# Queries and keys of batches 2 to 7: transposed by DMA instead of TensorE, with the bias columns appended to their token rows

## The chip, the cores and the metric

One core of one Trainium2 chip. The metric is the device time of one execution in microseconds (us). Every ratio below is the mean time of one kernel's fast runs over the mean of the other's fast runs of the same rounds, so it is not quite the ratio of the medians that are quoted beside it. "Fast" excludes executions in the chip's slower state. The "granted clock" is the share of TensorE's full clock that the profile shows as granted.

## The reference, cut to what matters

```python
# q, k, v: (8 batches, 8 heads, 576 tokens, 64);  s: (8, 8, 576)
scores = q @ k.T / 8
cum    = cumsum(max(s, 0))                       # per head, over tokens
bias   = min(-(cum[i] - cum[j]), 0)              # query i, key j
attn   = softmax(where(j > i, -1e9, scores + bias))
x      = concat_heads(attn @ v)                  # (8, 576, 512)
out    = x + relu(layernorm(x) * g @ w1) @ w2    # 512 -> 2048 -> 512
```

The bias is a difference of two vectors, so it can be carried by the score product itself: keys get the columns (c_hi, c_mid, c_lo, 1) and queries (1, 1, 1, -c), and the contraction grows from 64 to 68.

## The kernel before: the parts concerned

Everything runs as one software pipeline over n = 0 to 63, one step per head (n = 8 x batch + head). In each step TensorE (PE in the profile) does the scores of head n, the product with v of head n-1, and four "units" of the feed-forward network of the previous batch. Scores need q and k with the head dimension on the partitions; both arrive with tokens there, so they are transposed. In the kernel before TensorE does it, two heads at a time, and VectorE (DVE) copies the result from PSUM:

```python
def qk_pair(b, j):
    for kind, dst in (("k", kT), ("q", qT)):
        src = ready.pop((kind, b, j))                          # 96 x (6 x 2 x 64), bf16
        tr = ps_t.tile([P, S], BF16, name="trqk", tag="tr")    # ps_t: 2 buffers, tag "tr"
        for t in range(QT):                                    # 6 transposes
            nc.tensor.transpose(tr[:, t*QP:(t+1)*QP], src[0:QP, t], ident[0:QP, 0:QP])
        for u in range(2):                                     # 2 copies of 64 x 576
            copy_on("dve", dst[i][0:D, hh+u, 0:S]..., tr[u*D:(u+1)*D, :]...)

def aug(b, g, eng):            # the bias rows: four small DMAs per group of four heads
    for j, src in enumerate((c_hi, c_mid, c_lo)):
        eng.dma_start(out=kT[i][D+j:D+j+1, :, 0:S], in_=src[r0:r0+G, :])
    eng.dma_start(out=qT[i][D+3:D+4, :, 0:S], in_=c_neg[r0:r0+G, :])
# ... cut ...
def ln_tr(b, t):               # LayerNorm's own transposes use the same two PSUM buffers
    tr = ps_t.tile([P, KD, P], BF16, name="trx", tag="tr")
    ...
```

At the start of a batch, in the step of head 1, LayerNorm of the batch before stands on VectorE: statistics, reciprocal root (on GpSimd, POOL in the profile), five tiles xn, and then trx on TensorE. The output rows go out by

```python
def put(yo):
    nc.sync.dma_start(out=out[b, t*P:(t+1)*P, :], in_=yo)      # on SyncE's queue, at once
```

SyncE (SP, its queue SPq) issues all loads and stores, in program order (in the timeline of the changed kernel below, a store whose data is not there holds what stands behind it for 3.5 us).

The softmax here doesn't subtract the row's maximum and nothing guards it: scores larger than these inputs give would overflow.

## Time and profile before

| | before |
|---|---|
| time, median of the first three runs | 445.18 us (444.15 to 446.87) |
| span of the profiled run, mean granted TensorE clock | 445.4 us, 0.971 |
| TensorE / VectorE / ScalarE / GpSimd busy | 85 / 63 / 39 / 38% |
| DMA queue of SyncE, share of the 16 engines | 37.0% |
| a batch, first head to first head (batches 3 to 7) | 46.3 us |

A busy share is an average over the span; what sets the pace is read from how far apart the same instruction of successive heads lies, and from the waits of the engine that is full. Those views stand in the prediction.

### The profile page before, as it was taken

The page shows a single profiled execution, that of the slowest core. Times are in us where ns is not written, and L with a number is a line of the kernel's source. Part 1 is how long each engine was busy: PE and PEld are TensorE (multiplying, and loading weights), DVE is VectorE, ACT ScalarE, POOL GpSimd, SP SyncE. Part 2 cuts the span into 40 slices and gives each one's busy share as a digit, 9 for nine tenths or more (in the row PEclk, how much of TensorE's full clock was granted, in tenths as well). Part 3 has the DMA queues.
Part 4 walks back from the last instruction along what each step waited for, and adds up shares of the span by engine and source line. Part 5 has one row for each costly group of instructions (what it writes and reads, how often), then busy time and mean ns, then how long its engine had stood idle before and what let it go on. Part 6 is the DMA issues. An engine that isn't in the chain of part 4 may idle for free.

```text
span 445.4 us, 8185 instructions
## 1 busy us (share of the span) xinstructions
PE 377.6 (85%) x2973; PEld 208.6 (47%) x3024; DVE 280.8 (63%) x615; ACT 174.1 (39%) x339; POOL 171.4 (38%) x415
## 2 busy tenths in 40 slices
PE   1396459995999799969998899889997999999995
PEld 0174335553555455535554455445554554444442
DVE  8668787597656865775576767766668676411211
ACT  4164216631275136612762265215642560140420
POOL 4166514865445444442555255524444222000000
PEclk9999999997999899988999999969999999999999
DMA  7887075964531354134511551154221000101013
GB/s 198 214 231 199 10 243 174 271 197 119 143 107 55 101 149 115 29 96 129 142 56 52 162 152 54 53 149 125 71 76 47 26 1 24 72 0 72 24 26 71
DMA packets 61593, 47.13 MB, mean 106 GB/s; under 512 B 40232, under 2 KB 52784, under 8 KB 61552
## 3 DMA queue, kind: packets, MB, share of 16 engines
q1 hardware_dynamic: 61472, 46.56, 37.0%
q8 instruction: 24, 0.39, 0.4%
q14 instruction: 17, 0.14, 0.1%
q10 hardware_dynamic: 80, 0.05, 0.0%
HBM read 36.85 MB, written 9.44 MB: 104 GB/s over the span
## 4 chain that ended last, share of the span: by engine, by line
PE 65%; DVE 17%; issue 7%; POOL 5%; ACT 3%; DMA 1%; POOLq 0%; SPq 0%; ACTq 0%
PE ph L377 27%; PE py L395 21%; PE pot L289 4%; DVE xn L348 4%; DVE kT L108 4%; PE sa L213 3%; PE sb L213 3%; PE trqk L191 3%; DVE qT L108 3%; PE sc L213 2%; PE trx L364 2%; ACT hT L387 2%; POOL rs L335 2%; DVE yo L404 1%; POOL e L236 1%
## 5 line engine op out<-in xcount | busy, mean ns | idle before, releaser
L236 POOL TENSOR_SCALAR_AFFINE_SELECT e<-e 128x128 bf16<-128x128 bf16 x256 | 77.3, 315 | 169.4 <-ACT e L222 169.1
L395 PE MATMUL py<-w_bf,hT 128*128 128x512 bf16 x550 | 140.1, 392 | 1.9 <-issue 0.7
L377 PE MATMUL ph<-xT,w_bf 128*128 128x512 bf16 x489 | 121.3, 382 | 4.9 <-ACT hT L387 3.3
L387 ACT ACTIVATE hT<-ph 128x512 bf16<-128x512 f32 x108 | 64.5, 597 | 90.6 <-PE ph L377 86.1
L222 ACT ACTIVATE e<-sa 128x512 bf16<-128x512 f32 x64 | 38.1, 596 | 156.1 <-PE sa L213 145.7
L377 PEld LDWEIGHTS <-w_bf 128*128 128x128 bf16 x576 | 54.0, 98 | 59.9 <-issue 9.4
L395 PEld LDWEIGHTS <-hT 128*128 128x128 bf16 x576 | 54.3, 100 | 52.4 <-issue 4.6
L385 DVE TENSOR_SCALAR hT<-ph 128x512 bf16<-128x512 f32 x36 | 24.9, 692 | 46.4 <-PE ph L377 46.0
L108 DVE COPY kT<-trqk 64x576 bf16<-64x576 bf16 x62 | 46.6, 751 | 8.3 <-PE trqk L191 7.5
L289 PEld LDWEIGHTS <-e 128*128 128x128 bf16 x960 | 41.4, 103 | 16.7 <-issue 2.3
L108 DVE COPY qT<-trqk 64x576 bf16<-64x576 bf16 x64 | 48.3, 754 | 1.4
L289 PE MATMUL pot<-v_bf,e 128*128 128x65 bf16 x960 | 44.1, 201 | 4.0 <-POOL v_bf L110 3.4
L213 PEld LDWEIGHTS <-kT 68*128 68x128 bf16 x320 | 27.2, 106 | 37.3 <-issue 17.1
L297 DVE RECIPROCAL rinv<-pot 128x5 f32<-128x5 f32 x64 | 12.3, 193 | 46.6 <-PE pot L289 46.1
L364 PE MATMUL trx<-ident,xn 128*128 128x128 bf16 x144 | 16.3, 247 | 29.3 <-DVE kT L108 26.0
L222 ACT ACTIVATE e<-sc 128x512 bf16<-128x512 f32 x64 | 38.8, 606 | 0.0
L222 ACT ACTIVATE e<-sb 128x512 bf16<-128x512 f32 x64 | 38.0, 594 | 0.0
L213 PE MATMUL sa<-qT,kT 68*128 68x512 bf16 x64 | 27.7, 433 | 11.5 <-DMA qT<-c_neg 6.9
L404 DVE TENSOR_TENSOR yo<-py,xb 128x512 f32<-128x512 f32 x32 | 22.1, 690 | 24.3 <-PE py L395 24.1
L364 PEld LDWEIGHTS <-xn 128*128 128x128 bf16 x144 | 11.4, 110 | 39.7 <-DVE kT L108 29.0
L299 DVE TENSOR_TENSOR xb<-pot,rinv 128x256 f32<-128x256 f32 x64 | 27.2, 425 | 2.2
L110 POOL CAST qp<-qtmp 96x768 bf16<-96x768 f32 x31 | 26.2, 846 | 4.4 <-DMA qtmp<-in_q_dram 4.4
(56 smaller groups left out, 335.5 us busy)
## 6 DMA issues: line engine op xcount, KB each, us to landing
ktmp<-in_k_dram SPq DMA_DIRECT2D x32, 288.0 KB
qtmp<-in_q_dram SPq DMA_DIRECT2D x32, 288.0 KB
vtmp<-in_v_dram SPq DMA_DIRECT2D x32, 256.0 KB
out_dram<-yo SPq DMA_DIRECT2D x32, 256.0 KB
w1tmp<-in_moe_w_ch_dram SPq DMA_DIRECT2D x8, 512.0 KB
w2tmp<-in_moe_w_ch_dram SPq DMA_DIRECT2D x8, 512.0 KB
vtmp<-in_v_dram SPq DMA_DIRECT2D x8, 128.0 KB
out_dram<-yo SPq DMA_DIRECT2D x8, 128.0 KB
```

What stands on the lines that cost most here:

```text
L108: nc.vector.tensor_copy(out=out, in_=in_)
L110: nc.gpsimd.tensor_copy(out=out, in_=in_)
L213: nc.tensor.matmul(dst, lhsT=kk[0:KA, hh, kb * P : (kb + 1) * P], rhs=qq[0:KA, hh, q0:q1], start=True, stop=True,)
L222: nc.scalar.activation(out=e[:, u, o : o + 512], in_=a, func=ACT.Exp, scale=scale)
L236: nc.gpsimd.affine_select(out=e[:, u, o : o + P], in_=e[:, u, o : o + P], compare_op=ALU.is_ge, fill=0.0, base=0, pattern=[[1, P]], channe ...
L289: nc.tensor.matmul(pot[:, t, :], lhsT=e[:, u, o : o + P], rhs=vv[:, kb, h, :], start=(kb == 0), stop=(kb == last),)
L299: nc.vector.tensor_tensor(out=xb[b][:, :, hs], in0=pot[:, 0:NF, 0:D], in1=rinv[:, 0:NF].unsqueeze(2).to_broadcast([P, NF, D]), op=ALU.mult,)
L364: nc.tensor.transpose(tr[:, kd, :], xn[:, kd * P : (kd + 1) * P], ident)
L377: nc.tensor.matmul(ph, lhsT=w1_bf[:, kd, fb * P : (fb + 1) * P], rhs=xT[:, kd, :], start=(kd == 0), stop=(kd == KD - 1),)
L387: nc.scalar.activation(out=hT[:, fb, :], in_=ph, func=ACT.Relu)
L395: nc.tensor.matmul(py[0], lhsT=hT[:, fb, t * P : (t + 1) * P], rhs=w2_bf[:, fb, :], start=(fb == 0), stop=(fb == FB - 1),)
L404: nc.vector.tensor_add(out=yo, in0=py[0], in1=x)
```

## The change

Its intent: TensorE is the bound, so take the transposes from it, and with them VectorE's copies, which hold LayerNorm's transposes at each batch boundary. From batch 2 on (`NPE = 2`), q and k are loaded as tiles of 128 tokens x 4 heads, cast by GpSimd into rows of 128 columns per head (64 values, 4 bias columns, 60 zeros), and transposed by a DMA within SBUF. The bias then needs no DMAs of its own.

```diff
+    NPE = 2
+    PARTS = ((0, 1, 2), (3, 4))                 # token tiles; tile 4 is 64 tokens
-    xnp = ... bufs=6      +    xnp = ... bufs=5
-    e2 = 3 tiles of 2 heads     +    er = one tile of 4 heads
+    rows = [const.tile([P, G, P], BF16, name=f"rows{i}") for i in range(6)]
+    cTk, cTq: bias columns by token, made once at n == 6 (15 TensorE transposes, 4 DVE ops)
+
+    def ld_rows(kind, gam, part):               # gam: group of four heads
+        for u, t in enumerate(PARTS[part]):
+            nc.sync.dma_start(out=tmp[0:pn, u], in_=src[b, h0:h0+G, t*P:t*P+pn, :]...)
+    def cast_rows(kind, gam, part):
+            nc.gpsimd.tensor_copy(out=r[0:pn, :, 0:D], in_=tmp[0:pn, u])
+            nc.gpsimd.tensor_copy(out=r[0:pn, :, D:KA], in_=cTk or cTq ...)
+    def tr_rows(kind, gam, part):
+        for t, pn, r in ready.pop(...):
+            nc.sync.dma_start_transpose(out=dst[:, t*G*P : t*G*P + G*pn]..., in_=r[0:pn]...)
 # scores: the last 64 queries lie apart now, so three of five matmuls are cut in two
+        for a0, a1, cols in q_cols(b, h, q0, q1): nc.tensor.matmul(...)
 # per group of four heads, in the step of head n (the group is gam = n // 4 + 1):
+    n % 4 == 0:  tr k part 0;  cast q part 0;  load q part 1
+    n % 4 == 1:  tr q part 0;  cast k part 1;  load k part 0 of the next group
+    n % 4 == 2:  tr k part 1;  cast q part 1;  load q part 0 of the next group
+    n % 4 == 3:  tr q part 1;  cast and load k of the next group
-            qk_pair(g // 4, g % 4)
+            if g < 4 * NPE: qk_pair(g // 4, g % 4)
 # ... cut: loads and casts of the old form for batches 2 to 7, aug() beyond batch 1 ...
```

More of the change, by code (lines that the diff above doesn't have):

```diff
@@ L56 @@
     xpool = ctx.enter_context(tc.tile_pool(name="xpool", bufs=3))
-    xnp = ctx.enter_context(tc.tile_pool(name="xnp", bufs=6))
+    xnp = ctx.enter_context(tc.tile_pool(name="xnp", bufs=5))
     xtp = ctx.enter_context(tc.tile_pool(name="xtp", bufs=2))
@@ L76 @@
     kT = [const.tile([P, G, SP], BF16, name=f"kT{i}") for i in range(2)]
-    e2 = [const.tile([P, 2, EW], BF16, name=f"e2_{i}") for i in range(3)]
+    er = const.tile([P, 4, EW], BF16, name="er")
+    rows = [const.tile([P, G, P], BF16, name=f"rows{i}") for i in range(6)]
+    cTk = const.tile([P, NT, BH, 4], BF16, name="cTk")
+    cTq = const.tile([P, NT, BH, 4], BF16, name="cTq")
     xm = [const.tile([P, Dm], F32, name=f"xm{i}") for i in range(4)]
@@ L178, in aug, with bias_rows @@
         eng.dma_start(out=qT[i][D + 3 : D + 4, :, 0:S], in_=c_neg[r0 : r0 + G, :])
+    def bias_rows():
+        tr = ps_t.tile([P, 3, NT, BH], BF16, name="trc", tag="tr")
+        for j, src in enumerate((c_hi, c_mid, c_lo)):
+            for t in range(NT):
+                pn = P if t < NF else TL
+                nc.tensor.transpose(
+                    tr[0:pn, j, t, :], src[:, t * P : t * P + pn], ident[0:BH, 0:BH]
+                )
+        for t0, t1, pn in ((0, NF, P), (NF, NT, TL)):
+            nc.vector.tensor_copy(
+                out=cTk[0:pn, t0:t1, :, 0:3],
+                in_=tr[0:pn, :, t0:t1, :].rearrange("p j t x -> p t x j"),
+            )
+            nc.vector.tensor_scalar_mul(
+                out=cTq[0:pn, t0:t1, :, 3], in0=tr[0:pn, 0, t0:t1, :], scalar1=-1.0
+            )
@@ new lines, in ld_rows @@
+    def ld_rows(kind, gam, part):
+        if gam >= 2 * B:
+            return
+        src = k if kind == "k" else q
+        b, h0 = gam // 2, (gam % 2) * G
+        tmp = stage.tile([P, 3, G, D], F32, name=kind + "tmp", tag=kind + "tmp")
+        for u, t in enumerate(PARTS[part]):
+            pn = P if t < NF else TL
+            nc.sync.dma_start(
+                out=tmp[0:pn, u],
+                in_=src[b, h0 : h0 + G, t * P : t * P + pn, :].rearrange("h s d -> s h d"),
+            )
+        loaded[kind, gam, part, "rows"] = tmp
@@ new lines @@
+    turn = [0]
+    def cast_rows(kind, gam, part):
+        if gam >= 2 * B:
+            return
+        tmp = loaded.pop((kind, gam, part, "rows"))
+        got = []
+        for u, t in enumerate(PARTS[part]):
+            pn = P if t < NF else TL
+            r = rows[turn[0] % 6]
+            turn[0] += 1
+            nc.gpsimd.tensor_copy(out=r[0:pn, :, 0:D], in_=tmp[0:pn, u])
+            nc.gpsimd.tensor_copy(
+                out=r[0:pn, :, D:KA],
+                in_=(cTk if kind == "k" else cTq)[0:pn, t, gam * G : (gam + 1) * G, :],
+            )
+            got.append((t, pn, r))
+        ready[kind, gam, part, "rows"] = got
@@ L181, in qk_pair @@
+    def tr_rows(kind, gam, part):
+        if gam >= 2 * B:
+            return
+        dst = (kT if kind == "k" else qT)[gam % 2].rearrange("p h s -> p (h s)")
+        for t, pn, r in ready.pop((kind, gam, part, "rows")):
+            nc.sync.dma_start_transpose(
+                out=dst[:, t * G * P : t * G * P + G * pn].rearrange(
+                    "p (h s) -> p h s", h=G
+                ),
+                in_=r[0:pn].rearrange("p h c -> p (h c)"),
+            )
     def qk_pair(b, j, engs=("dve", "dve", "dve", "dve")):
@@ L204, in e_of, with k_cols, q_cols @@
     def e_of(b, h):
-        return e2[(b * 4 + h // 2) % 3], h % 2
+        return er, h % 4
+    def k_cols(b, h, kb):
+        i, hh = (b * 2 + h // G) % 2, h % G
+        if b < NPE:
+            return kT[i][0:KA, hh, kb * P : (kb + 1) * P]
+        n = P if kb < NF else TL
+        o = kb * G * P + hh * n
+        return kT[i].rearrange("p h s -> p (h s)")[0:KA, o : o + P]
+    def q_cols(b, h, q0, q1):
+        i, hh = (b * 2 + h // G) % 2, h % G
+        if b < NPE:
+            return [(q0, q1, qT[i][0:KA, hh, q0:q1])]
+        flat = qT[i].rearrange("p h s -> p (h s)")
+        got = []
+        if q0 < NF * P:
+            full = flat[0:KA, 0 : NF * G * P].rearrange("p (t h s) -> p t h s", t=NF, h=G)
+            got.append((q0, min(q1, NF * P), full[:, q0 // P : min(q1, NF * P) // P, hh, :]))
+        if q1 > NF * P:
+            o = NF * G * P + hh * TL
+            got.append((NF * P, q1, flat[0:KA, o : o + TL]))
+        return got
     def scores(b, h):
-        i, hh = (b * 2 + h // G) % 2, h % G
-        kk, qq = kT[i], qT[i]
         e, u = e_of(b, h)
         def mm(dst, kb, q0, q1):
-            nc.tensor.matmul(
-                dst,
-                lhsT=kk[0:KA, hh, kb * P : (kb + 1) * P],
-                rhs=qq[0:KA, hh, q0:q1],
-                start=True,
-                stop=True,
-            )
+            for a0, a1, cols in q_cols(b, h, q0, q1):
+                nc.tensor.matmul(
+                    dst[:, a0 - q0 : a1 - q0],
+                    lhsT=k_cols(b, h, kb),
+                    rhs=cols,
+                    start=True,
+                    stop=True,
+                )
         def ex(o, a):
@@ L246, in scores_d @@
     def scores_d(b, j):
-        i = (b * 2 + j // 2) % 2
-        e, _ = e_of(b, 2 * j)
+        e, u0 = e_of(b, 2 * j)
         d = ps_t.tile([P, 2, TL], F32, name="sd", tag="tr")
         for u in range(2):
-            hh = (2 * j + u) % G
             nc.tensor.matmul(
                 d[:, u, :],
-                lhsT=kT[i][0:KA, hh, NF * P : SP],
-                rhs=qT[i][0:KA, hh, NF * P : S],
+                lhsT=k_cols(b, 2 * j + u, NF),
+                rhs=q_cols(b, 2 * j + u, NF * P, S)[0][2],
                 start=True,
@@ L259, in scores_d @@
         nc.scalar.activation(
-            out=e[0:TL, :, OD : OD + TL], in_=d[0:TL], func=ACT.Exp, scale=scale
+            out=e[0:TL, u0 : u0 + 2, OD : OD + TL], in_=d[0:TL], func=ACT.Exp, scale=scale
         )
         nc.gpsimd.affine_select(
-            out=e[0:TL, :, OD : OD + TL],
-            in_=e[0:TL, :, OD : OD + TL],
+            out=e[0:TL, u0 : u0 + 2, OD : OD + TL],
+            in_=e[0:TL, u0 : u0 + 2, OD : OD + TL],
             compare_op=ALU.is_ge,
@@ L480 @@
         nc.gpsimd.memset(v_bf[i][0:TL, NF, :, D : D + 1], 1.0)
-    for i in range(3):
-        nc.gpsimd.memset(e2[i][TL:P, :, OD : OD + TL], 0.0)
-        nc.gpsimd.memset(e2[i][:, :, OD + TL : EW], 0.0)
+    nc.gpsimd.memset(er[TL:P, :, OD : OD + TL], 0.0)
+    nc.gpsimd.memset(er[:, :, OD + TL : EW], 0.0)
     cast("q", 0, 1, "pool")
@@ L546, in pre @@
             cast_w2(3), ld_w2(7)
-            ld("k", 2, 0), ld("q", 2, 0)
         elif n == 14:
@@ L552, in pre @@
             ld("v", 2, 1)
+            ld("v", 2, 2)
         elif n == 15:
-            cast("k", 2, 0, "pool")
-            cast("q", 2, 0, "pool")
-            ld("k", 2, 1), ld("q", 2, 1), ld("k", 2, 2), ld("q", 2, 2)
             cast("v", 2, 0, "pool")
-            ld("v", 2, 2)
+            ld("v", 2, 3)
         elif n == 16:
-            cast("k", 2, 1, "pool")
-            cast("q", 2, 1, "pool")
-            ld("k", 2, 3), ld("q", 2, 3)
             cast("v", 2, 1, "pool")
             cast("v", 2, 2, "pool")
-            ld("v", 2, 3), ld("v", 2, 4)
-        elif n > 16:
-            kind = "k" if n % 2 == 0 else "q"
-            g = (n + 2) // 2 if n % 2 == 0 else (n + 3) // 2
-            cast(kind, g // 4, g % 4, "pool")
-            ld(kind, (g + 2) // 4, (g + 2) % 4)
-            if n == 17:
-                cast("v", 2, 3, "pool")
-                cast("v", 2, 4, "pool")
-            if 1 <= h < 6 and b > 1:
+            ld("v", 2, 4)
+        elif n == 17:
+            cast("v", 2, 3, "pool")
+            cast("v", 2, 4, "pool")
@@ L575, in pre @@
+        if n == 4:
+            for r in rows:
+                nc.gpsimd.memset(r[:, :, KA:P], 0.0)
+        if n == 6:
+            nc.vector.memset(cTk[:, :, :, 3], 1.0)
+            nc.vector.memset(cTq[:, :, :, 0:3], 1.0)
+            bias_rows()
+        if n >= 17:
+            if 1 <= h < 6 and b + 1 < B:
                 ld("v", b + 1, h - 1)
-            if 3 <= h and b > 1:
+            if 3 <= h and b + 1 < B:
                 cast("v", b + 1, h - 3, "pool")
+        if n == 10:
+            ld_rows("k", 4, 0)
+        elif n == 11:
+            ld_rows("q", 4, 0)
+        elif n == 12:
+            cast_rows("k", 4, 0)
+            ld_rows("k", 4, 1)
+        elif n == 13:
+            tr_rows("k", 4, 0)
+            cast_rows("q", 4, 0)
+            ld_rows("q", 4, 1)
+            ld_rows("k", 5, 0)
+        elif n == 14:
+            tr_rows("q", 4, 0)
+            cast_rows("k", 4, 1)
+            ld_rows("q", 5, 0)
+        elif n == 15:
+            tr_rows("k", 4, 1)
+            cast_rows("q", 4, 1)
+            tr_rows("q", 4, 1)
+            cast_rows("k", 5, 0)
+            ld_rows("k", 5, 1)
+        elif n >= 16:
+            gam = n // 4 + 1
+            if n % 4 == 0:
+                tr_rows("k", gam, 0)
+                cast_rows("q", gam, 0)
+                ld_rows("q", gam, 1)
+            elif n % 4 == 1:
+                tr_rows("q", gam, 0)
+                cast_rows("k", gam, 1)
+                ld_rows("k", gam + 1, 0)
+            elif n % 4 == 2:
+                tr_rows("k", gam, 1)
+                cast_rows("q", gam, 1)
+                ld_rows("q", gam + 1, 0)
+            else:
+                tr_rows("q", gam, 1)
+                cast_rows("k", gam + 1, 0)
+                ld_rows("k", gam + 1, 1)
@@ L587 @@
             g = (n + 1) // 2
-            qk_pair(g // 4, g % 4)
+            if g < 4 * NPE:
+                qk_pair(g // 4, g % 4)
         scores(b, h)
@@ L598 @@
             pv(pb, ph_)
-            if ph_ == 3 and pb + 1 < B:
+            if ph_ == 3 and pb + 1 < NPE:
                 aug(pb + 1, 0, nc.sync)
-            if ph_ == 7 and pb + 1 < B:
+            if ph_ == 7 and pb + 1 < NPE:
                 aug(pb + 1, 1, nc.sync)
```

## The prediction

> **What bounds the kernel now.** I read the summary first, then the waits of the matmul engine, then the timeline around one batch boundary, then the chain of work. The summary and the strip of forty slices:
>
> ```profile
> PE 377.6 (85%) x2973; PEld 208.6 (47%) x3024; DVE 280.8 (63%) x615; ACT 174.1 (39%) x339; POOL 171.4 (38%) x415
> ...
> PE   1396459995999799969998899889997999999995
> ```
>
> PE is busy nearly everywhere from the seventh slice on, with a dent every four or five slices; no other engine is above 63%. The start times of successive first score matmuls (tile sa) in the timeline lie 4.96 and 5.14 us apart in turn, regular to 0.05 us, so inside a batch PE alone sets the pace. The first head of batches 3, 4, 5, 6 and 7 starts at 142.08, 187.18, 235.33, 279.21 and 327.43 us: 46.3 us a batch on average. The dents are named by PE's waits:
>
> ```profile
> PE trx L364 <- DVE kT L108: 26.0, 7, 7.8
> PE sa L213 <- DMA qT<-c_neg: 6.9, 1, 6.9
> ```
>
> (Columns: total us, times, longest.) Seven stalls, 26 us, are waits of the LayerNorm transposes (trx) for the copies of transposed keys out of PSUM. One of them, in the timeline:
>
> ```profile
> 284.11 0.42 PE L191 MATMUL trqk<-ident,qp 96*128 96x96 bf16 x6
> ...
> 285.08 1.17 POOL L335 TENSOR_TENSOR rs<-rs,mhalf 128x5 f32<-128x5 f32 x1 [2.95 <-DVE rs L334]
> ...
> 286.29 2.40 DVE L348 TENSOR_SCALAR xn<-xb,mv,rs 128x512 bf16<-128x512 f32 x4 [1.29 <-POOL rs L335]
> ...
> 289.17 0.69 DVE L404 TENSOR_TENSOR yo<-py,xb 128x512 f32<-128x512 f32 x1
> ...
> 289.78 1.51 DVE L108 COPY kT<-trqk 64x576 bf16<-64x576 bf16 x2
> ...
> 291.35 0.61 PE L364 MATMUL trx<-ident,xn 128*128 128x128 bf16 x4 [3.98 <-DVE kT L108]
> ...
> 295.59 0.63 PE L213 MATMUL sa<-qT,kT 68*128 68x512 bf16 x1
> ```
>
> PE put both query/key transposes into the two PSUM buffers that trx also uses, at 283.85 and 284.11. VectorE empties them only after LayerNorm statistics, the reciprocal root on POOL, five xn and one output add. So trx waits until 291.35, though its operand xn was there by 287.0. Finally the chain of work shows what the query/key transposes cost where PE is full:
>
> ```profile
> 228.24 0.46 PE pot L289 x15
> ...
> 230.42 0.51 PE trqk L191 x12
> ```
>
> Twelve transposes (one pair of heads, keys and queries) take 0.51 us; fifteen matmuls of 65 columns take 0.46, 31 ns each, with their weight loads hidden.
>
> [...] after the 4 us stall above, four 512-column matmuls are 0.43 us apart instead of 0.216, and sa starts at half speed at 295.59. [...] SyncE takes 0.38 to 0.47 us per load[...]. For the transposes no run yet shows anything. [...] The kernel before has none.
>
> **The change part by part.** Batches 2 to 7 are 48 heads, 24 pairs.
>
> Removed from PE: 24 x 0.51 = 12.3 us. All of it is on the path, since PE is saturated within batches.
>
> Removed from VectorE: 24 x 4 copies x 0.754 us (the rows of kT and qT copies) = 72 us. Inside a batch that is hidden. At the boundary it is not. I measured each boundary by the step from the sa of head 1 to that of head 2 and the next. Without stall the first should last about 4.99 (scores 0.65, three further mlp units of 0.86 and the first one, pot 0.46, two trx of 0.22), the second about 5.8. Found: 10.48 and 8.09, 9.58 and 5.60, 11.22 and 7.04, 8.37 and 5.59, 11.23 and 7.09, 8.37 and 5.6. The losses, half clock included, are 7.8, 4.6, 7.5, 3.4, 7.5, 3.4: 34.2 us in six boundaries. In the changed kernel no trqk holds the buffers. In the boundary shown PE would reach trx at 287.37 - 0.51 = 286.9, and xn is ready at about 287.0. What remains is head 2's sd tile, which needs the first trx buffer back: VectorE must do the other xn (to 289.14), the output add (to 289.86), the three pot operations (0.9 us) and one xT copy (0.42), so 291.2, while PE gets there at about 290.6. I leave 0.7 us of loss per boundary: 34.2 - 4.2 = 30.0 us saved.
>
> Added on PE: the tail tile of queries lies apart, so three score matmuls of each of 48 heads are cut in two. The columns stay the same; a 64-column piece costs 31 ns against the 27 it saved, so 144 x 4 ns = 0.6 us. The 15 bias transposes at head 6 are about 0.6 us.
>
> Added on VectorE, at head 6 and where it is 79% busy (20 to 60 us): copies and scalings of about 1000 elements and two strided memsets, by the rate of the kT copy (576 in 0.75 us) about 3 us. I charge 2.
>
> POOL: loads of 96x768 cast in 0.82 us, of 128x512 in 0.61, so about 0.2 + 0.8 ns per element. A 128x256 row tile is then 0.41, and the 16-element bias copy about 0.2: per group of four heads 10 x 0.61 = 6.1 us instead of 4 x 0.82 = 3.3. Twelve groups add 34 us to 171; half busy, and each cast is queued one head ahead of its transpose. Hidden.
>
> DMA: key and query rows become 256-byte packets. The trace's packets of that size took 18 ns and those of 1536 B 86 ns, so 55,296 x 18 / 16 = 63 us of all engines in place of 9,216 x 86 / 16 = 49. The 120 transposes move 15 MB more; at the same 18 ns per 256 B that is about 60 us. The share goes from 37% to some 58%: not a bound by itself. The 48 small bias DMAs (0.57 us of issue each) vanish.
>
> SyncE is the open term. Per batch it issues 20 row loads x 0.4 + 5 v loads x 0.47 + 4 stores x 0.38 = 12 us, and 20 transposes of T each. [...] So 29 to 40 us per batch, against PE's 46.3 - 2.05 - 5.0 + 0.1 = 39.4. It fits, barely.
>
> Sum: 445.2 - 12.3 - 30.0 + 1.2 + 2 = 406. For the tightness of SyncE I add 4: **410 us**.
>
> **The rivals.** (a) SyncE becomes the bound. With T = 1.7 a batch needs 46 us and all is given back (about 445); with T = 2.0 it needs 52, and six batches give +34, some 480; at 3 us it is 600. For it: it is in-order, and a store that waits for VectorE stops the transposes behind it (SyncE waited 122 us for output adds in the kernel before). Against: that waiting is slack, used only when it is early. (b) The transposes land late. Each group's last query transposes are issued one head (5 us) before the first matmul that needs them. If cast, issue and landing take 7, PE waits 2 us in each of 12 groups, partly at half clock: about 435. The order of instructions shows that every DMA also waits for the one eight places before, so latencies can chain. (c) Another link takes over at the boundary (the xT copy, POOL's reciprocal root behind longer casts), and only 3 of 7 us go there on average: about 420. (d) [...] it was 0.97 with the stalls, so I expect no less.
>
> **Range and chances.** If T is at most 1.4 (I give it 0.6) the time is 398 to 425. Between 1.4 and 1.8 (0.15) it is 420 to 450. Above (0.25) it is slower, to 480 and beyond. So 398 to 480 for 8 in 10; faster by over 2% 0.63, within 2% 0.09, slower 0.28.
>
> **What would show it right or wrong.** Right: no trqk rows after batch 1; PE's waits for trx at the six later boundaries below 1 us each; distance of first heads 39 to 40 us; VectorE's busy time near 212 us, POOL's near 205; transposes that hold SyncE 0.8 to 1.4 us. Wrong: PE's weight loads of kT waiting for DMAs at every fourth head, SyncE issuing without pause, transposes of over 1.7 us, or a landing time above 5 us.

## The result, and the profile after

The changed kernel is slower: 470.5 us (467.65 to 473.01, 4 runs) against 444.88 us of the kernel before in the same rounds; ratio 1.0566, 95% interval 1.0485 to 1.0648. The record marks the runs built on this kernel as correct, all but e3, which is wrong. The profiled run: span 466.9 us, granted clock 0.893.

The summary and the strip of the changed kernel:

```profile
PE 371.4 (80%) x2848; PEld 200.3 (43%) x2895; DVE 213.3 (46%) x525; ACT 175.4 (38%) x339; POOL 193.2 (41%) x609
...
PE   1486469917979984999299939896699899999995
```

Less work on TensorE and VectorE, as intended, but new holes in the strip: the 2 and the 3 and the 6s. What TensorE waits for:

```profile
PE sa L305 <- DMA qT<-rows: 47.3, 8, 10.2
PE trx L454 <- DVE kT L113: 7.8, 1, 7.8
```

The LayerNorm waits are gone but for the one at n = 9, in batch 1, which the change does not touch. In their place the first score matmul of a group waits 47.3 us in all for transposed queries, eight times.

To see where the time went, I took the start of each head's first score matmul (sa) in both traces and compared the 63 steps between them:

| steps | before to after, us |
|---|---|
| start of the first sa | +0.7 |
| n = 0 to 9 (the bias transposes are at n = 6) | +1.6 |
| the twelve steps of the six batch boundaries (n = 17, 18, 25, 26, ... 58) | -33.6 |
| the two steps around each group's start (n = 15, 16, 19, 20, 27, 28, 35, 36, ... 60), without the boundaries | +59.2 |
| the other 27 steps | -6.2 |
| sum, to the sa of n = 63 | +21.7 |

After the last sa nothing differs by more than 0.2 us. So the change did what it was for, and lost it again at the group starts. They are not alike: the second group of a batch, whose first head is head 4, waits 7.0 to 8.6 us in batches 3 to 6 (8.3, 8.6, 7.0, 8.5), and the first group of a batch at most 0.5 in batches 3 to 7 (counted from 0). Here is one of the long ones, in the timeline of the changed kernel (start, duration, engine; SPq is what SyncE issues):

```profile
206.94 0.38 PE L305 MATMUL sa<-qT,kT 68*128 68x512 bf16 x1
...
209.37 2.40 DVE L438 TENSOR_SCALAR xn<-xb,mv,rs 128x512 bf16<-128x512 f32 x4 [1.28 <-POOL rs L425]
...
210.03 0.40 PE L454 MATMUL trx<-ident,xn 128*128 128x128 bf16 x4
...
212.21 0.38 PE L305 MATMUL sa<-qT,kT 68*128 68x512 bf16 x1
...
212.48 0.69 DVE L494 TENSOR_TENSOR yo<-py,xb 128x512 f32<-128x512 f32 x1
...
213.20 0.37 SPq L507 DMA_DIRECT2D out_dram<-yo  x1
...
214.15 3.96 SPq L243 DMA_TRANSPOSE qT<-rows  x3
...
218.08 0.38 PE L305 MATMUL sa<-qT,kT 68*128 68x512 bf16 x1
218.16 2.46 SPq L213 DMA_DIRECT2D ktmp<-in_k_dram  x3
220.72 0.45 SPq L507 DMA_DIRECT2D out_dram<-yo  x1
221.75 2.82 SPq L243 DMA_TRANSPOSE kT<-rows  x2
224.63 1.67 SPq L213 DMA_DIRECT2D qtmp<-in_q_dram  x3
226.40 0.45 SPq L507 DMA_DIRECT2D out_dram<-yo  x1
...
227.42 2.70 SPq L243 DMA_TRANSPOSE qT<-rows  x2
...
231.41 0.58 PE L305 MATMUL sa<-qT,kT 68*128 68x512 bf16 x1 [8.61 <-DMA qT<-rows]
```

First, trx at 210.03 has no wait any more: the step of head 1 takes 5.27 us (206.94 to 212.21), where it took 11.22 in the kernel before. Second, the store at 213.20. SyncE had finished issuing at 209.7 (its loads before) and then stood still for 3.5 us, because in its queue the next thing was an output store, whose data VectorE makes at 212.48 only, after LayerNorm's xn. Third, the store, the last query transpose and what lies between them are nineteen issues, and they end at 230.1: 16.9 us. TensorE needs only two steps for heads 34 and 35 (212.21 + 5.87 + 4.57 = 222.65). It waits, and goes on at a lower clock: the step of n = 36 lasts 7.43 us instead of 4.64, at a mean granted clock of 0.61.

Each transpose holds SyncE for 1.2 us in the median, twice as long as a row load:

```profile
L243 SPq DMA_TRANSPOSE kT<-rows x60: 1181/1207/2378, 83.6 to 368.7; - x60
L243 SPq DMA_TRANSPOSE qT<-rows x60: 1186/1217/2714, 93.8 to 371.9; - x60
L213 SPq DMA_DIRECT2D ktmp<-in_k_dram x60: 419/573/1305, 67.4 to 351.9; - x60
L213 SPq DMA_DIRECT2D qtmp<-in_q_dram x60: 367/573/1491, 73.5 to 358.9; - x60
```

(Least, median and largest duration in ns.) I added up SyncE's instructions from the sa of head 24 to that of head 56, four batches. Per batch, 20 transposes (1.33 us in the mean), 20 row loads (0.57), five v loads (0.49) and four stores (0.43) are 42.4 us; the short pauses between issues, 0.04 to 0.22 us each, are another 3.7; and SyncE stands still for longer than 0.3 us at a time for 3.5, nearly all of it before stores. Together these are 49.6 us, which is the length of a batch. TensorE needs some 39 (a batch of e8, below, takes 39.3). So SyncE is too slow even where it does not stand still: its 46.1 us do not fit into 39.

### The profile page after: what moved, and what is told of

The parts are those of the page before. It is cut to its first block, busy times and chain, and to the rows that moved or that the text cites. A ratio compares the mean times of both kernels' runs of the same rounds, so it can differ in the third digit from the quotient of the medians.

```text
span 466.9 us, 8307 instructions
## 1 busy us (share of the span) xinstructions
PE 371.4 (80%) x2848; PEld 200.3 (43%) x2895; DVE 213.3 (46%) x525; ACT 175.4 (38%) x339; POOL 193.2 (41%) x609
## 2 busy tenths in 40 slices
DMA packets 167578, 61.09 MB, mean 131 GB/s; under 512 B 155624, under 2 KB 158768, under 8 KB 167536
## 3 DMA queue, kind: packets, MB, share of 16 engines
q1 hardware_dynamic: 167456, 60.51, 57.1%
## 5 line engine op out<-in xcount | busy, mean ns | idle before, releaser
L328 POOL TENSOR_SCALAR_AFFINE_SELECT er<-er 128x128 bf16<-128x128 bf16 x256 | 73.4, 303 | 87.4 <-ACT er L314 86.9
L314 ACT ACTIVATE er<-sa 128x512 bf16<-128x512 f32 x64 | 38.1, 596 | 166.1 <-PE sa L305 107.3
L305 PEld LDWEIGHTS <-kT 68*128 68x128 bf16 x464 | 35.8, 105 | 95.2 <-issue 38.2
L305 PE MATMUL sa<-qT,kT 68*128 68x512 bf16 x64 | 27.8, 434 | 60.2 <-DMA qT<-rows 47.3
L379 PEld LDWEIGHTS <-er 128*128 128x128 bf16 x960 | 42.7, 105 | 17.9 <-issue 5.2
L379 PE MATMUL pot<-v_bf,er 128*128 128x65 bf16 x960 | 45.1, 203 | 3.2 <-POOL v_bf L115 2.5
L230 POOL CAST rows<-qtmp 128x256 bf16<-128x256 f32 (+1 forms) x60 | 24.1, 401 | 46.8 <-issue 25.1
L387 DVE RECIPROCAL rinv<-pot 128x5 f32<-128x5 f32 x64 | 12.4, 193 | 61.2 <-PE pot L379 61.0
L494 DVE TENSOR_TENSOR yo<-py,xb 128x512 f32<-128x512 f32 x32 | 22.0, 689 | 39.5 <-PE py L485 39.3
L314 ACT ACTIVATE er<-sc 128x512 bf16<-128x512 f32 x64 | 38.9, 608 | 0.0
L314 ACT ACTIVATE er<-sb 128x512 bf16<-128x512 f32 x64 | 38.2, 596 | 1.8 <-PE sb L305 0.7
L230 POOL CAST rows<-ktmp 128x256 bf16<-128x256 f32 (+1 forms) x60 | 23.9, 399 | 25.7 <-DMA kT<-rows 17.3
L305 PE MATMUL sb<-qT,kT 68*128 68x384 bf16 (+2 forms) x176 | 28.4, 269 | 2.5 <-DMA qT<-rows 2.3
L305 PE MATMUL sc<-qT,kT 68*128 68x256 bf16 (+1 forms) x224 | 28.5, 249 | 0.0
```

Of the source, the lines that this page charges most:

```text
L230: nc.gpsimd.tensor_copy(out=r[0:pn, :, 0:D], in_=tmp[0:pn, u])
L305: nc.tensor.matmul(dst[:, a0 - q0 : a1 - q0], lhsT=k_cols(b, h, kb), rhs=cols, start=True, stop=True,)
L314: nc.scalar.activation(out=e[:, u, o : o + 512], in_=a, func=ACT.Exp, scale=scale)
L328: nc.gpsimd.affine_select(out=e[:, u, o : o + P], in_=e[:, u, o : o + P], compare_op=ALU.is_ge, fill=0.0, base=0, pattern=[[1, P]], channe ...
L379: nc.tensor.matmul(pot[:, t, :], lhsT=e[:, u, o : o + P], rhs=vv[:, kb, h, :], start=(kb == 0), stop=(kb == last),)
L494: nc.vector.tensor_add(out=yo, in0=py[0], in1=x)
```

## The experiments

Three theories stood at the start. A: a store that waits for VectorE at the batch boundary holds the transposes behind it in SyncE's queue. B: SyncE is simply full. (When I wrote the expectations I reckoned with 37 us of issue per batch of 39, because I had taken a row load at 0.42 us and left out the pauses; the trace has 46.1.) C: the transposes land late, because the DMA engines are loaded (57.1% after against 37.0% before). All kernels were run against the kernel before, in the same rounds.

**e1: stores deferred.** Each store of batches 0 to 6 is put into the queue one head later, behind that head's transposes and loads.

```diff
-                nc.sync.dma_start(out=out[b, t*P:(t+1)*P, :], in_=yo)
+                held.append((out[b, t*P:(t+1)*P, :], yo))
...
         pre(n)
+        flush()          # issues what is held
```

> Edit: each output store of batches 0 to 6 is put on SyncE's queue after the transposes and loads of the next head instead of at once; same instructions otherwise. Theory A (a store that waits at the batch boundary for VectorE holds the query transposes behind it): the waits of sa for DMA qT at heads 28, 36, 44 and 52 (8.3, 8.6, 7.0, 8.5 us) fall below 2 us, each with some 2.5 us of half clock, so about 425 to 435 us. Theory B (SyncE is full anyway: some 37 us of issue per batch of 39): little changes, 455 to 468. Theory C (the transposes land late because the DMA engines are loaded): unchanged, 465 to 472.

Measured: 452.11 us, ratio 1.0141 (1.0098 to 1.0184). The waits at heads 28, 36, 44 and 52 fell from 8.3, 8.6, 7.0 and 8.5 us to 4.9, 3.9, 4.4 and 3.4. None of the three expectations was met: the store is a cause, since moving it alone is worth 18 us, but half the stall stays. In this run SyncE stands still for 0.2 us per batch only, and its issues and short pauses fill 45.7 us of a batch of 46.0: without the held store SyncE itself sets the pace, which is the sign of being wrong that the prediction called "SyncE issuing without pause".

**e2: row loads on another queue.** The loads of q and k rows are issued from ScalarE's queue.

```diff
-            nc.sync.dma_start(          # in ld_rows
+            nc.scalar.dma_start(
```

> Edit: the row loads of keys and queries (20 per batch, 0.42 us of issue each) are issued from ScalarE's queue; stores stay where they are. Theory A alone: the store still holds the transposes at the boundary, but SyncE has 8.4 us per batch less to issue, so it catches up before head 4: stalls of 1 to 4 us, 430 to 445. Theory B: 415 to 430, the stalls mostly gone. Theory C: unchanged, 460 or more. ScalarE may be slowed by 8.4 us per batch of issue at 38% busy, which should not show.

Measured: 453.48 us (one of the four runs was slow), ratio 1.0155 (1.0104 to 1.0205). Its profile was slow, so I read only the places of the waits from it: heads 28, 36, 44 and 52 still wait 3.8 to 5.4 us. Again a part of the stall, less than A or B had said. And against my expectation ScalarE did feel it: TensorE waits 8.5 us in eleven places for ScalarE's relu (0.5 us in two places in the changed kernel), which stands behind row loads in ScalarE's order.

**e3: plain copies in place of the transposes.** Same bytes, same tiles, wrong result (relative error 0.89), the bias columns zeroed so that nothing overflows.

```diff
-            nc.sync.dma_start_transpose(out=dst[...], in_=r[0:pn]...)
+            nc.sync.dma_start(out=dst[...], in_=r[:, :, 0:pn])
```

> Edit: each of the 120 transposes is replaced by a plain copy of the same bytes between the same tiles (wrong result on purpose; the bias columns are zeroed so that nothing overflows). Theories A and B: each issue falls from 1.2 to about 0.4 us, 16 us per batch are freed, the stalls at heads 4 vanish but for the first group: 405 to 415. Theory C (movement and landing, not issue): the bytes and packets are as before, so the stalls stay at over half: 450 or more.

Measured: 442.01 us, ratio 0.9906 (0.9859 to 0.9952). This was the run that surprised me. A plain copy holds SyncE for 0.55 us in the median (least 0.47) instead of 1.2, yet heads 28, 36, 44 and 52 still wait 6.0, 5.3, 3.8 and 5.3 us. The timeline of this run at the same place as above:

```profile
201.17 0.69 DVE L495 TENSOR_TENSOR yo<-py,xb 128x512 f32<-128x512 f32 x1
...
201.89 0.36 SPq L508 DMA_DIRECT2D out_dram<-yo  x1
...
202.83 1.95 SPq L244 DMA_DIRECT2D qT<-rows  x3
...
212.92 1.36 SPq L244 DMA_DIRECT2D qT<-rows  x2
...
216.79 0.58 PE L306 MATMUL sa<-qT,kT 68*128 68x512 bf16 x1 [5.29 <-DMA ktmp<-in_k_dram]
```

(The profile names a key load as what ended the last wait, though sa reads only qT and kT; I read from the line the length of the wait alone.) The held store is still there, and the same nineteen issues take from 201.89 to 214.3, 12.4 us, even when each is cheap; heads 34 and 35 leave 10.4. So the length of an issue is not the whole of it, and theory B alone falls: SyncE's issues and pauses now need 32.1 us per batch, and it stands still for 11.8. Theory C has not been excluded by this run: the bytes move as before, though in fewer packets (134,938 against 167,578).

**e4: one transpose for three tiles.** The three tiles of part 0 lie in one buffer and are transposed by one instruction.

```diff
-    rows = 6 tiles of [P, G, P]
+    rows = 2 tiles of [P, 3, G, P]
+            nc.sync.dma_start_transpose(
+                out=dst[:, t0*G*P:(t0+m)*G*P].rearrange("p (x s) -> p x s", x=m*G),
+                in_=r[:, 0:m].rearrange("p t h c -> p (t h c)"))
```

> Edit: the three row tiles of a part lie in one buffer and are transposed by one instruction (128x1536) instead of three; part two keeps a full and a half tile. If the 1.2 us are per instruction (a half tile took as long as a full one), SyncE issues 12 instead of 20 transposes per batch, 9.6 us less: theory B 415 to 430, theory A 425 to 445. If they are per block of 128 columns, the merged ones take 3.6 us each and the time is unchanged, 462 to 475. A merged transpose also waits for three casts instead of one, up to 1.2 us later.

Measured: 452.07 us, ratio 1.0138 (1.0102 to 1.0174). SyncE's queue in this run:

```profile
200.87 1.57 SPq L213 DMA_DIRECT2D qtmp<-in_q_dram  x2
208.17 0.36 SPq L510 DMA_DIRECT2D out_dram<-yo  x1
...
230.11 1.34 SPq L244 DMA_TRANSPOSE qT<-rows  x1
...
234.99 1.20 SPq L249 DMA_TRANSPOSE kT<-rows  x1
```

The transpose at 230.11 moves 128x1536 in 1.34 us and the one at 234.99 half a tile, 64x512, in 1.20. These are near the least; the 24 transposes of 128x1536 take 1.86 us in the median (1.34 to 4.50), against some 3.6 for three single ones. So most of the cost is per instruction, and merging gives SyncE back 7.9 us per batch (46.1 to 38.2). The first two lines show where that went: SyncE was done at 202.4 and stood still until 208.17 for the store. More than half of the freed time was turned into waiting for stores (SyncE stands still for 8.1 us per batch instead of 3.5), and the stalls stayed at 5.2 to 6.9 us. Theories A and B each describe half: the store sets when the queue starts again, the issues behind it set how long the last query tile takes.

If that is so, both edits together must give far more than either.

**e5: deferred stores and loads on ScalarE's queue** (e1 and e2 together).

> Edit: both former edits together, stores deferred and row loads issued from ScalarE; 20 single transposes per batch stay. If held stores and SyncE's issue time are the two causes and add, the stalls at heads 28, 36, 44, 52 (3.4 to 4.9 us with the deferral alone, 3.8 to 5.4 with the loads moved alone) fall below 2 us: 430 to 440. If a third thing (landing times, POOL's six row buffers) holds the last query tiles, they stay at 3 us or more: 445 to 452.

Measured: 431.77 us, ratio 0.9662 (0.9618 to 0.9706), as expected of two causes that add. The only wait for transposed queries left is 1.7 us at head 16. The same bytes cross the same DMA engines here, so theory C falls with this run: the transposes did not land late because the engines were loaded. The price of ScalarE's queue shows: TensorE waits 16.8 us for ScalarE's relu.

**e6: deferred stores and merged transposes** (e1 and e4 together).

> Edit: merged transposes (12 instead of 20 per batch, each still about 1.2 us by the last run) and deferred stores. Two causes that add: stalls at those four heads under 1 us, only the one at head 16 (7.5 us and half clock) stays: 418 to 430. A third cause in landing or buffers: 440 to 452.

Measured: 422.68 us, ratio 0.9442 (0.9375 to 0.9508). Alone, each edit was worth 18 us against the changed kernel; together they are worth 48. Left are 7.9 us at head 16 and 2.0, 2.3, 1.3 and 2.6 at heads 28, 36, 44 and 52.

**e7: an earlier start for the first transposed group** on top of e6. The rows of heads 16 to 19 are loaded from n = 10 on together, and two casts of batch 1 move from n = 12 to 10 to free the buffers.

```diff
+        if n == 10:  ld_rows("k", 4, 0);  ld_rows("q", 4, 0)
+        elif n == 11: cast_rows("k", 4, 0);  ld_rows("k", 4, 1);  ld_rows("q", 4, 1)
+        elif n == 12: tr_rows("k", 4, 0);  cast_rows("q", 4, 0);  ld_rows("k", 5, 0)
 # ... n = 13 to 15 in the same manner; from 16 on as before
```

> Edit: as the run before, and the loads, casts and transposes of the first transposed group (heads 16 to 19) are begun one to two heads earlier. If the stall at head 16 comes from that group's late start behind weight loads and casts, it goes: some 8 to 10 us less than the merged and deferred kernel, 408 to 420. If it comes from elsewhere: the same time as that one.

Measured: 419.99 us, ratio 0.9361 (0.9315 to 0.9407). The wait at head 16 fell from 7.9 to 4.3 us, but the gain is smaller than I had expected, and the interval overlaps that of e6: it is not shown to be faster. In this kernel the order inside a step is v loads, transposes, row loads, store; at the boundary the deferred store still waits 2 us.

**e8: transposes first.** On top of e7, each head's transposes are the first thing that SyncE issues for that head.

```diff
     def pre(n):
+        if n >= 16:  tr_rows("kqkq"[n % 4], n // 4 + 1, n % 4 // 2)     # ahead of everything
 # ... and taken out of their former places
```

> Edit: on top of merged, deferred and early: each head's transposes are the first thing SyncE issues for that head, ahead of the v load and the deferred store, which at the batch boundary still wait 2 us for VectorE's output add. If what is left (1.7 to 2.9 us at heads 28, 36, 52, 4.3 at head 16) is still queue order on SyncE, it falls below 1 us but at head 16: 405 to 415. If it is POOL's casts behind the reciprocal root, or the two row buffers: unchanged, 417 to 422.

**e10: the same with the store issued at once**, as in the changed kernel.

```diff
-                held.append((out[b, t*P:(t+1)*P, :], yo))
+                nc.sync.dma_start(out=out[b, t*P:(t+1)*P, :], in_=yo)
```

> Edit: as the run before, but with each store issued at once as in the changed kernel, so after the head's transposes and loads and ahead of the next head's transposes. If the held store is what matters, the stalls at heads 28 to 52 come back to 3 to 6 us: 430 to 445. If the order of transposes within a head is enough: 405 to 418.

Measured, five rounds each: e8 413.99 us, ratio 0.9278 (0.9244 to 0.9312); e10 441.85 us, ratio 0.9904 (0.987 to 0.9938). The two differ in nothing but where the store stands in SyncE's queue: 28 us. Their timelines at the second boundary step; first e10:

```profile
200.19 0.38 PE L308 MATMUL sa<-qT,kT 68*128 68x512 bf16 x1
...
200.96 0.37 SPq L510 DMA_DIRECT2D out_dram<-yo  x1
201.43 1.50 SPq L244 DMA_TRANSPOSE qT<-rows  x1
...
216.14 0.58 PE L308 MATMUL sa<-qT,kT 68*128 68x512 bf16 x1 [5.57 <-DMA qT<-rows]
```

and e8:

```profile
184.74 1.82 SPq L244 DMA_TRANSPOSE qT<-rows  x1
...
190.17 0.38 PE L308 MATMUL sa<-qT,kT 68*128 68x512 bf16 x1
...
191.16 0.36 SPq L513 DMA_DIRECT2D out_dram<-yo  x1
191.62 1.21 SPq L244 DMA_TRANSPOSE kT<-rows  x1
...
201.61 0.38 PE L308 MATMUL sa<-qT,kT 68*128 68x512 bf16 x1 [0.84 <-DMA qT<-rows]
```

The first query transpose is issued 1.2 us after the sa of n = 34 in e10 and 5.4 us before it in e8, and the stall of 5.57 us becomes 0.84. The strip of e8 has no holes from the twelfth slice on:

```profile
PE   1288716996899999999999999998999999999994
```

and in its waits transposed queries are left with 3.6 us in all, three times, 2.6 of them once (at head 16):

```profile
PE sa L308 <- DMA qT<-rows: 3.6, 3, 2.6
```

By the table of steps, e8 against the kernel before: first sa -0.4, n = 0 to 9 +5.0, boundaries -33.7, group starts +2.8, the rest -7.9, in all -34.3 us. Its batches are 40.3, 38.3, 39.4 and 38.8 us long (sa of heads 28, 36, 44, 52, 60). This version beats both kernels.

The same sum over SyncE's instructions as above, from the sa of head 24 to that of head 56, for all runs (us per batch):

| run | issues and short pauses | standing still | batch |
|---|---|---|---|
| changed kernel | 46.1 | 3.5 | 49.6 |
| e1, store deferred | 45.7 | 0.2 | 46.0 |
| e2, loads on ScalarE (slow) | 32.5 | 12.4 | 47.7 |
| e3, plain copies | 32.1 | 11.8 | 45.9 |
| e4, merged | 38.2 | 8.1 | 47.1 |
| e10, as e7 with transposes first, but store at once | 37.0 | 7.8 | 45.8 |
| e5, deferred, loads on ScalarE | 32.9 | 9.3 | 42.5 |
| e6, merged and deferred | 39.5 | 1.6 | 41.3 |
| e7, e6 with an earlier start | 39.0 | 1.8 | 41.0 |
| e8, as e10 with store deferred | 37.5 | 2.1 | 39.3 |

Either edit alone leaves SyncE late: full without a long pause (e1), or with about half or more of the freed time spent standing still, chiefly before stores (e2, e3, e4, e10). Only both together bring a batch near TensorE's 39 us. (In e5 SyncE has time to spare, and TensorE's waits for ScalarE lengthen the batch.)

## Why the prediction was wrong, point by point

*TensorE's share: right, and larger than reckoned.* No trqk is left after batch 1. The boundaries gave 33.6 us, of which six times 0.51 are the transposes themselves; the other 30.5 stand against the 30.0 worked out. The steps of heads without a boundary fell from 4.96 and 5.14 us (the last head of a batch has 4.56, which the prediction did not mention) to 4.57 and 4.64: 0.89 us per pair of heads inside a batch, where 0.51 was reckoned. The split score matmuls cost nothing that can be seen.

*VectorE and GpSimd: right.* 213.3 us busy (predicted near 212) and 193.2 (predicted 205). GpSimd's casts took 0.39 us and the bias copies 0.19.

*The DMA engines: right, and not a bound.* 57.1% (predicted 58%); the packets of 256 bytes kept 18 ns in the median (mean 19.7). e5 showed that the same traffic lets the stalls vanish.

*The duration of a transpose: the size was right, the reason wrong.* The "0.8 to 1.4 us" held (1.2 in the median, 1.33 in the mean). But it was an estimate of mine in which the cost grows with the blocks of the tile, and no trace of the kernel before shows a DMA transpose. The least durations in e4 are 1.19 us for half a tile, 1.19 for a tile and 1.34 for three, so it is chiefly the instruction that costs. Had I known, the first thing to try would have been one wide transpose. The landing time, above 5 us a sign of being wrong, is given by one profile, that of e2 (slow): 2.4 us from issue to landing in the median for key tiles and 3.6 for query tiles.

*The step that failed* is the sum for SyncE, "29 to 40 us per batch, against PE's ... 39.4. It fits, barely", together with the sentence against rival (a), "that waiting is slack, used only when it is early". The 29 to 40 rested on T from 0.85 to 1.4 us, an estimate that nothing measured supported then. A batch takes SyncE 46.1 us: the transposes stayed within that range, but a row load took 0.57 us where 0.4 was put in (3.5 us per batch), and the pauses between issues (3.7 us) were not in the sum. On top of that it stood still for 3.5 us per batch, nearly all before stores. Together that is 49.6 us, 10.2 more than the 39.4, or 41 us over the four batches counted; the steps at their group starts grew by 39.8 us. (Of the 59.2 in the table of steps, 12.6 belong to head 16, in the start-up, which stays open.) In the kernel before, the waiting is slack: SyncE waited 122 us for output adds, and none of TensorE's long waits in batches 2 to 7 was for a DMA. In the changed kernel, what stands behind the store has a deadline two to three heads off: the stretch from the held store to the last query transpose took 16.9 us, and the two heads in it 10.4. Rival (a) was closest. It set 46 us per batch and "about 445" at T = 1.7; the 46 us were reached at T = 1.2 to 1.33, and e1, without the store's hold, took 452. It had named the store in the in-order queue too, but gave it no size. The 4 us added "for the tightness of SyncE" stood for a term that measured 59 us.

*Rival (b)* saw the other end of the same thing, a late last query transpose, and its wrong part was "2 us in each of 12 groups": it is 7 to 10 us in five of them, and 2.9 or less in the others. (The wait of a DMA for the one eight places before is in the trace of the kernel before: SyncE's issues use eight semaphores in turn, and 201 of the 218 wait for their own. What it costs was not measured.) *Rival (c)* did not happen. *The granted clock* of (d), "0.97 with the stalls", fell to 0.89, but after the new stalls and not from denser work: at heads 16, 20, 28, 36, 44 and 52 it is 1.0 over the 4 us before the stall and 0.59 to 0.65 in the step after it. In e8, with TensorE denser than in any other run (87% busy), it is 0.99. The length of a stall alone did not tell whether a slower step followed: in e7 the step after a stall of 1.92 us at head 36 took 6.29 us instead of 4.64 (four feed-forward matmuls in 1.90 us), while in e6 the step after one of 2.33 us at the same head took 4.66 (four in 1.03).

e8, with the queue in order, wide transposes and an earlier first group, takes 414 us, near the predicted 406 to 410. That nearness is in part luck: the gain per pair of heads was larger than reckoned, and the steps of n = 0 to 9, where 2.6 us more were reckoned, took 5.0 more.

What stays open: the 10.2 us at head 16 of the changed kernel were lowered by e7 and e8 (to 2.6) but not taken apart; weight loads and casts of the start-up share SyncE and GpSimd there. Whether GpSimd's row buffers (it waits 37.5 us for transposes to free them) prolong the chain was not tested; in the changed kernel SyncE stood still before a transpose for 0.4 us in the four batches counted. What makes some transposes last more than twice the median (2.7 us against 1.2) is open as well.

## What to carry to other kernels

A queue that issues in order, as SyncE's does here, has a sum per batch (46.1 us, where TensorE needs some 39) and a deadline for each entry, and both must fit. Take the sum from measured issues of the very shape, with the pauses between them; a load of another shape misled here by 0.17 us, twenty times per batch. Then, before work with a near deadline is put on a queue, look for the entries on it that wait for their data, and reckon from the moment that such a wait ends. Put what is waited for soon ahead of stores, and give stores a place where their data is surely there (441.9 us against 414.0 by the place of the store alone). And when two edits gain little one by one, ask whether one's gain is spent on the other's cause: here 18 and 18 us became 48 together.
